# Sorted v of three batches: natural-layout sort and a re-tiling by way of DRAM in place of TensorE transposes

## The chip, the cores and the metric

The kernel runs on one core of one Trainium2 chip. The metric is the device time of one run in microseconds (us), given as the median of several runs. Profiles are of one run each, and their span is some 2 us shorter than that run's time, as it counts from the first to the last instruction.

## The reference

```python
# q, k, v: (4, 8, 768, 64); sort_net: (4, 8, 8, 8); w_in (512, 2048), w_out (2048, 512)
P = sort_net                        # 5 rounds of exp and row/column normalisation
k_sorted = einsum('bhij,bhjcd->bhicd', P, k_blocks)    # 8 blocks of 96 rows
v_sorted = einsum('bhij,bhjcd->bhicd', P, v_blocks)
scores = q_block @ k_sorted_block.T / 8                # block by block
out = softmax(scores) @ v_sorted_block
x = out with heads side by side                        # (3072, 512)
y = square(relu(x @ w_in)) @ w_out                     # the feed-forward part
```

Attention-times-v needs each sorted v block with its 96 rows on the partitions. The loads put 6 neighbouring rows of v side by side on one partition, so partition (j, c) holds rows 6c to 6c+5 of block j.

## The kernel before

A plan on the host orders the work of TensorE, ScalarE and VectorE once and for all: the attention pieces of four batches are woven between chunks of feed-forward matmuls. Batch 0 runs partly ahead. A head pair ("unit") of a later batch does this for v:

```python
def s_sort(u, t, due=0, early=False):          # t = 1: k, t = 2: v
    for a in range(NA):                        # 6
        for h in range(2):
            nc.tensor.matmul(                  # output transposed: head dim on partitions
                out=tp[64 * h:64 * (h + 1), a, :],
                lhsT=src[:, 2 * u.hp + h, D * a:D * (a + 1)],
                rhs=w_all[...])                # the sorting matrix moves
    # evicted to ksT or vsT
...
def s_vt(u, due=0):                            # v only: eight transposes back
    for n in range(u.ni):
        nc.tensor.transpose(out=vbp[:, n, :], in_=u.vsT[...], identity=ident)
    # evicted to vs, the right operand of attention-times-v (s_av)
...
def load(b, t, h0, n, p=slice(0, 128)):        # bulk loads, cast to bf16, issued by GpSimd
    ...                                        # for b > 1 they wait until batch b-2 is read out
```

In the profiles `tp` is the sort's output, `vbp` the transposes', `scp` the scores, `oup` attention-times-v, `xtp` the transposes of the attention output, `hp` the up- and `op` the down-projection.

The softmax here doesn't subtract the row's maximum and nothing guards it: scores larger than these inputs give would overflow.

Of the kernel before, what the change touches and what calls it, by code (L numbers as in the profile page):

```python
# [8 lines left out]
FP32 = mybir.dt.float32  # L9
BF16 = mybir.dt.bfloat16  # L10
# [32 lines left out]
class Plan:  # L43
# [1 line left out]



    TAIL = {"PE": 0.0, "ACT": 0.09, "DVE": 0.06, "POOL": 0.0, "DMA": 0.0, "SP": 0.0}
    HOP = 0.06

    def __init__(self):
# [60 lines left out]
def kernel(  # L112
# [10 lines left out]
    nc = tc.nc  # L123
# [24 lines left out]


    ctx.enter_context(tc.manual_schedule(engines={  # L150
        mybir.EngineType.PE, mybir.EngineType.DVE, mybir.EngineType.Activation}))

    plan = Plan()
    r1, r2, rf, rh1, rh2, rob = Ring(1), Ring(2), Ring(3), Ring(3), Ring(2), Ring(3)
    rqT, rao, rks, ret = Ring(6), Ring(3), Ring(3), Ring(4)
    AD = ("ACT", "DVE")

    def cost_f(n):
        return (0.17 + 0.82e-3 * n, 0.15 + 1.04e-3 * n)
# [26 lines left out]

    ksT_r, vsT_r, et_r, vs_r = [], [], [], []
    for n in range(3):
        for r, name in ((ksT_r, "ksT"), (vsT_r, "vsT")):
            sT = const.tile([128, 2, HS + 32], BF16, name=f"{name}{n}")  # L190
            nc.vector.memset(sT[:, :, HS:HS + 32], 0.0)
            r.append(sT)
        vs = const.tile([96, NB, 2, 66], BF16, name=f"vs{n}")
        nc.vector.memset(vs[:, :, :, D:D + 1], 1.0)
        vs_r.append(vs)
    for n in range(4):
        et = const.tile([96, 2, HS + 32], BF16, name=f"et{n}")
        nc.vector.memset(et[:, :, HS:HS + 32], 0.0)
        et_r.append(et)
# [46 lines left out]
        t = slice(NT // 4 * g, NT // 4 * (g + 1))  # L246
        dma(("w_out", g), 1.05, lambda t=t: (w_out_bf[:, t, :], w_out_r[:, t, :]))
    for g in range(2):
        for t in (1, 2, 0):
            load(1, t, HP * g, HP)  # L250


# [136 lines left out]
    def s_sort(u, t, due=0, early=False):  # L389

        st = {}

        def mm(e):
            src = qkv[u.b][t]
            if early:
                tp = psf.tile([128, 512], FP32, tag="pf", name="tp")
                tp = tp[:, 0:NA * u.ni * C0].rearrange("p (a x) -> p a x", a=NA)
            else:
                tp = ps2.tile([128, NA, u.ni * C0], FP32, tag="p2", name="tp")
            st["p"] = tp  # L400
            for a in range(NA):
                for h in range(2):
                    nc.tensor.matmul(  # L403
                        out=tp[64 * h:64 * (h + 1), a, :],
                        lhsT=src[:, 2 * u.hp + h, D * a:D * (a + 1)],
                        rhs=w_all[:, H * u.b + 2 * u.hp + h, u.i0:u.i0 + u.ni, :]
                        .rearrange("p i c -> p (i c)"),
                        start=True, stop=True)

        def ev(e):  # L410
            h0 = u.halves[0]
            copy(e, (u.ksT if t == 1 else u.vsT)[:, h0:h0 + len(u.halves), 0:HS]
                 .rearrange("p h (x a) -> p h x a", a=NA),
                 st["p"].rearrange("p a (h x) -> p h x a", x=NQ * C0))

        h0 = 2 * u.hp
        dep = landed[u.b, t, h0 if u.b == 0 else HP * (h0 // HP), 0]
        ring = rf if early else r2
        s2, old = ring.take()
        pe = plan.add("PE", 0.385 if u.full else 0.27, mm,  # L420
                      [dep, built[H * u.b + h0], built[H * u.b + h0 + 1]] + old, due)
        readers[u.b].append(pe)
        op = plan.add(AD, cost_f(NA * C0 * u.ni), ev, [pe] + u.old)
        ring.use(s2, pe, op)
        return op

    def s_sc(u, due=0):

        u.exps = {}
        u.et, last = {}, []  # L430
        for hf in u.halves:
            st = {}

            def mm(e, hf=hf, st=st):
                qT = tiles["qT", u.b, u.hp]
                st["p"] = scp = ps2.tile([128, 2, 512], FP32, tag="p2", name="scp")
                for n in range(NQ):
                    for h in range(2):
                        nc.tensor.matmul(  # L439
                            out=scp[:, h, BLK * n:BLK * (n + 1)],  # L440
                            lhsT=u.ksT[64 * h:64 * (h + 1), hf, BLK * n:BLK * n + 128],
                            rhs=qT[64 * h:64 * (h + 1), NQ * hf + n, :, :]
                            .rearrange("p a c -> p (a c)"),
                            start=True, stop=True)

            s2, old = r2.take()
            u.et[hf], olde = ret.take()
            pe = plan.add("PE", 0.25, mm, [u.k_op, u.q_op] + old, due)
            r2.use(s2, pe)
            rqT.use(qTs[u.b, u.hp], pe)  # L450
            last.append(pe)
            u.exps[hf] = []
            for h in range(2):
                def ex(e, h=h, st=st, et=et_r[u.et[hf]]):
                    nc.scalar.activation(  # L455
                        out=et[:, h, 0:HS].rearrange("p (n c a) -> p n c a", c=C0, a=NA),
                        in_=st["p"][0:96, h, 0:HS].rearrange("p (n a c) -> p n c a", c=C0, a=NA),
                        func=AF.Exp, scale=scale)
                op = plan.add("ACT", cost_f(HS)[0], ex, [pe] + olde)
                r2.use(s2, op)  # L460
                u.exps[hf].append(op)
        u.sc_pe = last

    def s_vt(u, due=0):

        st = {}

        def mm(e):
            st["p"] = vbp = ps1.tile([128, u.ni, 128], BF16, tag="p1", name="vbp")
            for n in range(u.ni):  # L470
                i = u.i0 + n
                nc.tensor.transpose(  # L472
                    out=vbp[:, n, :],
                    in_=u.vsT[:, i // NQ, BLK * (i % NQ):BLK * (i % NQ) + 128],
                    identity=ident)

        def ev(e):
            copy(e, u.vs[:, u.i0:u.i0 + u.ni, :, 0:D],
                 st["p"][0:96].rearrange("p n (e d) -> p n e d", d=D))

        s1, old = r1.take()
        pe = plan.add("PE", 0.446 if u.full else 0.22, mm, [u.v_op] + old, due)
        u.vs_op = plan.add(AD, cost_b(128 * u.ni), ev, [pe] + u.old)
        r1.use(s1, pe, u.vs_op)
        rks.use(u.n, pe, *u.sc_pe)

    def s_av(u, due=0):
        nao, olda = rao.take()
        u.norms = []
        for hf in u.halves:  # L490
            st = {}

            def mm(e, hf=hf, st=st):
                if hf == u.halves[0]:
                    u.ao = att.tile([96, u.ni, 2, D], BF16, tag="ao", name="ao", bufs=3)
                st["p"] = oup = ps2.tile([128, 2, 512], FP32, tag="p2", name="oup")
                for n in range(NQ):
                    for h in range(2):
                        nc.tensor.matmul(  # L499
                            out=oup[:, h, 66 * n:66 * n + D + 1],  # L500
                            lhsT=et_r[u.et[hf]][:, h, BLK * n:BLK * n + 128],
                            rhs=u.vs[:, NQ * hf + n, h, 0:D + 1],
                            start=True, stop=True)

            def norm(e, st=st, n0=NQ * hf - u.i0):
# [12 lines left out]
            op = plan.add("DVE", 0.9, norm, [pe])  # L518
            r2.use(s2, pe, op)
            ret.use(u.et[hf], pe)  # L520
            rks.use(u.n, pe)
            u.norms.append(op)
        u.nao = nao

# [123 lines left out]
    def lay(b, halves, c0, c1):  # L648
        step = (c1 - c0) / (HP + 0.9)
        for hp in range(HP):  # L650
            c = c0 + step * hp
            box = {}

            def open_(due, b=b, hp=hp, box=box):
                u = box["u"] = Unit(b, hp, halves)
                u.q_op = s_q(b, hp, C0 * u.i0, C0 * (u.i0 + u.ni), due)
                if b > 0:
                    build_w(H * b + 2 * hp, 2, pt, kops[b - 1, hp])
                u.k_op = kops[b, hp] = s_sort(u, 1, due)
                u.v_op = s_sort(u, 2, due)  # L660

            for f, s in ((0.0, open_),
                         (0.35, lambda due, box=box: s_sc(box["u"], due)),
                         (0.5, lambda due, box=box: s_vt(box["u"], due)),
                         (0.75, lambda due, box=box: s_av(box["u"], due)),
                         (1.2, lambda due, box=box: s_xt(box["u"], due))):
                todo.append((c + step * f, len(todo), s, b))

    lay(0, (1,), 0, n_up)
    for b, (c0, c1) in enumerate(((n_up, 2 * n_up), (2 * n_up, 4 * n_up), (4 * n_up, 6 * n_up)), 1):  # L670
# [2 lines left out]
    for due, _, stage, b in sorted(todo, key=lambda x: x[:2]):  # L673
        if b > 1 and not readers[b]:
            for g in range(2):
                for t in (1, 2, 0):
                    load(b, t, HP * g, HP)
        stage(int(due))
    for g in range(n_tok // HS):
# [41 lines left out]
```

## Time and profile before

| | before |
|---|---|
| time, median | 241.75 us (241.41 to 242.11, 3 runs); 241.88 with the run beside the changed kernel |
| span of the profiled run | 238.9 us (that run's time was 241.00 us, below the four in the row above) |
| TensorE busy | 230.5 us (96%) |
| VectorE, ScalarE busy | 51% each |
| bulk loads (software queue) | 13.63 MB, of which the later batches' run until about 62 us and from 73 to 90 us |

The prediction below shows the lines and how they are read.

### The profile page before, as it was taken

The page shows a single profiled execution, that of the slowest core. Times are in us where ns is not written, and L with a number is a line of the kernel's source. Part 1 is how long each engine was busy: PE and PEld are TensorE (multiplying, and loading weights), DVE is VectorE, ACT ScalarE, POOL GpSimd, SP SyncE. Part 2 cuts the span into 40 slices and gives each one's busy share as a digit, 9 for nine tenths or more (in the row PEclk, how much of TensorE's full clock was granted, in tenths as well). Part 3 has the DMA queues.
Part 4 walks back from the last instruction along what each step waited for, and adds up shares of the span by engine and source line. Part 5 has one row for each costly group of instructions (what it writes and reads, how often), then busy time and mean ns, then how long its engine had stood idle before and what let it go on. Part 6 is the DMA issues. An engine that isn't in the chain of part 4 may idle for free.

```text
span 238.9 us, 5867 instructions
## 1 busy us (share of the span) xinstructions
PE 230.5 (96%) x2485; PEld 138.1 (58%) x2501; DVE 121.4 (51%) x322; ACT 123.0 (51%) x256; POOL 27.0 (11%) x41
## 2 busy tenths in 40 slices
PE   7899999999999999999999999999999999999993
PEld 2777665556675556655665456655665456446541
DVE  6677777327785347744676037643666025105400
ACT  4365675237885247724674147723674147227510
POOL 8843221500006000000000000000000000000000
PEclk9999999999999999999999999999999999999999
DMA  6999999999405990011100120011100120011012
GB/s 81 193 204 207 206 207 206 201 241 222 76 3 68 220 238 9 3 44 47 45 3 0 44 91 0 3 44 47 44 3 1 47 88 1 19 72 44 0 44 88
DMA packets 20489, 20.30 MB, mean 85 GB/s; under 512 B 1008, under 2 KB 17392, under 8 KB 20464
## 3 DMA queue, kind: packets, MB, share of 16 engines
q0 software_dynamic: 16960, 13.63, 36.8%
q1 hardware_dynamic: 3504, 6.30, 7.2%
q8 instruction: 19, 0.31, 0.5%
q14 instruction: 6, 0.05, 0.1%
HBM read 27.27 MB, written 6.29 MB: 140 GB/s over the span
## 4 chain that ended last, share of the span: by engine, by line
PE 91%; DVE 4%; ACT 2%; issue 1%; POOL 0%; POOLq 0%
PE hp L562 35%; PE op L590 34%; PE tp L403 5%; PE vbp L472 3%; PE qtp L361 3%; PE oup L499 3%; PE scp L439 3%; PE xtp L531 3%; ACT qT L166 1%; DVE p_sb L266 1%; PE fill L283 0%; DVE vs L168 0%; ACT h L570 0%; DVE rs L265 0%; POOL qb L212 0%
## 5 line engine op out<-in xcount | busy, mean ns | idle before, releaser
L562 PE MATMUL hp<-xT,w_in_bf 128*128 128x384 bf16 x512 | 92.8, 326 | 0.0
L590 PE MATMUL op<-w_out_bf,h 128*128 128x512 bf16 x368 | 86.2, 379 | 1.0 <-issue 0.3
L570 ACT ACTIVATE h<-hp 128x384 bf16<-128x384 f32 x128 | 62.3, 494 | 26.1 <-PE hp L562 25.4
L573 DVE TENSOR_TENSOR h<-h 128x384 bf16<-128x384 bf16 x128 | 43.9, 354 | 37.2 <-ACT h L570 36.7
L562 PEld LDWEIGHTS <-w_in_bf 128*128 128x128 bf16 x512 | 46.4, 98 | 28.1
L590 PEld LDWEIGHTS <-h 128*128 128x128 bf16 x384 | 36.1, 98 | 39.7
L166 ACT COPY ob<-op 128x512 f32<-128x512 f32 x24 | 14.1, 586 | 57.5 <-PE op L590 57.5
L455 ACT ACTIVATE et<-scp 96x384 bf16<-96x384 f32 x64 | 26.4, 490 | 6.7 <-PE scp L439 6.7
L509 DVE TENSOR_TENSOR ao<-oup,rec 96x512 bf16<-96x512 f32 x32 | 22.0, 687 | 1.1
L168 DVE COPY vs<-vbp 96x1024 bf16<-96x1024 bf16 (+1 forms) x20 | 11.6, 580 | 19.5 <-PE vbp L472 19.4
L168 DVE COPY qT<-qtp 128x768 bf16<-128x768 bf16 (+1 forms) x15 | 7.3, 489 | 18.9 <-PE qtp L361 18.4
L166 ACT CAST ksT<-tp 128x768 bf16<-128x768 f32 (+1 forms) x17 | 11.7, 686 | 9.9 <-PE tp L403 9.6
L168 DVE COPY xT<-xtp 128x768 bf16<-128x768 bf16 (+1 forms) x16 | 7.9, 496 | 13.3 <-PE xtp L531 12.8
L283 PE MATMUL fill<-ones 128*128 128x128 bf16 (+1 forms) x108 | 12.0, 255 | 1.5 <-DVE ones L185 1.5
L499 PEld LDWEIGHTS <-et 96*128 96x128 bf16 x256 | 10.7, 98 | 3.1 <-ACT h L570 0.6
L168 DVE CAST vsT<-tp 128x768 bf16<-128x768 f32 (+1 forms) x14 | 11.8, 840 | 0.8
L499 PE MATMUL oup<-vs,et 96*128 96x65 bf16 x256 | 11.6, 193 | 0.2 <-DVE vs L168 0.2
L361 PEld LDWEIGHTS <-qb 128*64 128x64 bf16 (+1 forms) x240 | 6.9, 109 | 7.1 <-issue 5.8
L508 DVE RECIPROCAL rec<-oup 96x8 f32<-96x8 f32 x32 | 6.4, 199 | 8.3 <-PE oup L499 8.1
L472 PE MATMUL vbp<-ident,vsT 128*128 128x128 bf16 x128 | 10.5, 219 | 0.0
L212 POOL DMA_DIRECT2D qb<-in_q_dram x8 | 6.0, 747 | 39.1 <-PE qtp L361 33.3
L361 PE MATMUL qtp<-ident,qb 128*64 128x128 bf16 (+1 forms) x240 | 9.3, 212 | 0.8 <-DVE qT L168 0.4
(48 smaller groups left out, 130.5 us busy)
## 6 DMA issues: line engine op xcount, KB each, us to landing
out_dram<-ob SPq DMA_DIRECT2D x24, 256.0 KB, 2.0
qb<-in_q_dram POOLq DMA_DIRECT2D x8, 384.0 KB, 12.4
kb<-in_k_dram POOLq DMA_DIRECT2D x6, 384.0 KB, 15.1
vb<-in_v_dram POOLq DMA_DIRECT2D x6, 384.0 KB, 16.3
w_in_bf<-in_moe_w_in_dram POOLq DMA_DIRECT2D x4, 512.0 KB, 13.2
w_out_bf<-in_moe_w_out_dram POOLq DMA_DIRECT2D x4, 512.0 KB, 19.3
kb<-in_k_dram POOLq DMA_DIRECT2D x4, 192.0 KB, 6.1
vb<-in_v_dram POOLq DMA_DIRECT2D x4, 192.0 KB, 6.4
```

What stands on the lines that cost most here:

```text
L166: nc.scalar.copy(out=out, in_=in_)
L168: nc.vector.tensor_copy(out=out, in_=in_)
L283: nc.tensor.matmul(out=tiles["fill"][:, 0:w], lhsT=ones[:, 0:128], rhs=ones[:, 0:w], start=True, stop=True)
L361: nc.tensor.transpose(out=t["p"][64 * h:64 * (h + 1), a, :], in_=qb[p0:p1, 2 * hp + h, D * a:D * (a + 1)], identity=ident[p0:p1, p0:p1])
L455: nc.scalar.activation(out=et[:, h, 0:HS].rearrange("p (n c a) -> p n c a", c=C0, a=NA), in_=st["p"][0:96, h, 0:HS].rearrange("p (n a c) - ...
L472: nc.tensor.transpose(out=vbp[:, n, :], in_=u.vsT[:, i // NQ, BLK * (i % NQ):BLK * (i % NQ) + 128], identity=ident)
L499: nc.tensor.matmul(out=oup[:, h, 66 * n:66 * n + D + 1], lhsT=et_r[u.et[hf]][:, h, BLK * n:BLK * n + 128], rhs=u.vs[:, NQ * hf + n, h, 0:D ...
L509: nc.vector.tensor_tensor(out=u.ao[:, n0:n0 + NQ, :, :].rearrange("p n e d -> p e n d"), in0=ov[:, :, :, 0:D], in1=rec[:, :, :, None].to_b ...
L562: nc.tensor.matmul(out=t["hp", nt][:, 0:HS], lhsT=w_in_bf[:, kc, 128 * nt:128 * (nt + 1)], rhs=xT[:, kc, t0:t0 + HS], start=(kc == 0), sto ...
L570: nc.scalar.activation(out=t["h1", nt], in_=t["hp", nt][:, 0:HS], func=AF.Relu)
L573: nc.vector.tensor_tensor(out=t["h2"][:, nt, :], in0=t["h1", nt], in1=t["h1", nt], op=ALU.mult)
L590: nc.tensor.matmul(out=t["op", mt], lhsT=t["h2"][:, nt, 128 * mt:128 * (mt + 1)], rhs=w_out_bf[:, nt, :], start=(nt == 0), stop=(nt == NT ...
```

## The change

The intent is to take the eight transposes per unit off TensorE, which is the bound. For batches 1 to 3 the sorting matrix becomes the stationary operand and v moves in its natural layout. The result is written to DRAM and read back with the block rows on the partitions. A block holds two units (four heads).

```diff
+    def s_vn(b, g, due):
+        for hp in (2 * g, 2 * g + 1):
+            for h in range(2):
+                nc.tensor.matmul(out=st["p"][:, h, 0:NA * D],
+                    lhsT=w_all[:, H * b + 2 * hp + h, :, :]...,      # 128 columns stationary
+                    rhs=qkv[b][2][:, 2 * hp + h, :], ...)            # 384 columns moving
+            # evicted to vn, then:
+        nc.sync.dma_start(out=v_way[b, g], in_=vn ...)               # 396 KB
+        nc.sync.dma_start(out=vb_r[w] ...,                           # 768 pieces of 528 B
+                          in_=v_way[b, g].rearrange("(i c) a x -> (c a) i x", c=C0))
 ...
-            for t in (1, 2, 0):
+            for t in (2, 1, 0):                                      # v is loaded first
 ...
+            if b > 0 and hp % 2 == 0:
+                todo.append((max(c - 7, 0), len(todo), v_first, b))  # 7 chunks ahead
-                u.v_op = s_sort(u, 2, due)
+                if b == 0:
+                    u.v_op = s_sort(u, 2, due)
```

The sync engine's order, too, is now fixed by the plan, which counts 2.3 us for a write and 2.6 us for a read.

More of the change, by code (lines that the diff above doesn't have):

```diff
@@ L43 @@
 class Plan:
-    TAIL = {"PE": 0.0, "ACT": 0.09, "DVE": 0.06, "POOL": 0.0, "DMA": 0.0, "SP": 0.0}
+    TAIL = {"PE": 0.0, "ACT": 0.09, "DVE": 0.06, "POOL": 0.0, "DMA": 0.0, "SP": 0.0, "WAY": 0.0}
     HOP = 0.06
@@ L150 @@
     ctx.enter_context(tc.manual_schedule(engines={
-        mybir.EngineType.PE, mybir.EngineType.DVE, mybir.EngineType.Activation}))
+        mybir.EngineType.PE, mybir.EngineType.DVE, mybir.EngineType.Activation,
+        mybir.EngineType.SP}))
     plan = Plan()
+    rvn, rvb = Ring(2), Ring(3)
     r1, r2, rf, rh1, rh2, rob = Ring(1), Ring(2), Ring(3), Ring(3), Ring(2), Ring(3)
@@ L188 @@
     for n in range(3):
-        for r, name in ((ksT_r, "ksT"), (vsT_r, "vsT")):
-            sT = const.tile([128, 2, HS + 32], BF16, name=f"{name}{n}")
+        for r, name, hs in ((ksT_r, "ksT", 2), (vsT_r, "vsT", 1)):
+            sT = const.tile([128, hs, HS + 32], BF16, name=f"{name}{n}")
             nc.vector.memset(sT[:, :, HS:HS + 32], 0.0)
             r.append(sT)
-        vs = const.tile([96, NB, 2, 66], BF16, name=f"vs{n}")
+        vs = const.tile([96, NQ, 2, 66], BF16, name=f"vs{n}")
         nc.vector.memset(vs[:, :, :, D:D + 1], 1.0)
         vs_r.append(vs)
+    vn_r, vb_r = [], []
+    for n in range(2):
+        vn = const.tile([128, NA, HP, 66], BF16, name=f"vn{n}")
+        nc.vector.memset(vn[:, :, :, D:66], 1.0)
+        vn_r.append(vn)
+    for n in range(3):
+        vb_r.append(const.tile([96, NB, HP, 66], BF16, name=f"vblk{n}"))
+    v_way = nc.dram_tensor("v_way", (B, 2, 128, NA, HP * 66), BF16, kind="Internal").ap()
     for n in range(4):
@@ L410, in ev @@
         def ev(e):
-            h0 = u.halves[0]
+            h0 = u.halves[0] if t == 1 else 0
             copy(e, (u.ksT if t == 1 else u.vsT)[:, h0:h0 + len(u.halves), 0:HS]
@@ L429, in s_sc @@
         u.exps = {}
-        u.et, last = {}, []
+        u.et = {}
         for hf in u.halves:
@@ L450, in s_sc @@
             rqT.use(qTs[u.b, u.hp], pe)
-            last.append(pe)
+            rks.use(u.n, pe)
             u.exps[hf] = []
@@ L461, in s_sc @@
                 u.exps[hf].append(op)
-        u.sc_pe = last
     def s_vt(u, due=0):
@@ L473, in mm @@
                     out=vbp[:, n, :],
-                    in_=u.vsT[:, i // NQ, BLK * (i % NQ):BLK * (i % NQ) + 128],
+                    in_=u.vsT[:, 0, BLK * (i % NQ):BLK * (i % NQ) + 128],
                     identity=ident)
         def ev(e):
-            copy(e, u.vs[:, u.i0:u.i0 + u.ni, :, 0:D],
+            copy(e, u.vs[:, :, :, 0:D],
                  st["p"][0:96].rearrange("p n (e d) -> p n e d", d=D))
@@ L484, in s_vt, with mm, ev, write @@
         r1.use(s1, pe, u.vs_op)
-        rks.use(u.n, pe, *u.sc_pe)
+        rks.use(u.n, pe)
+    v_blk = {}
+    def s_vn(b, g, due):
+        m, oldm = rvn.take()
+        evs = []
+        for hp in (2 * g, 2 * g + 1):
+            st = {}
+            def mm(e, hp=hp, st=st):
+                st["p"] = ps2.tile([128, 2, 512], FP32, tag="p2", name="vnp")
+                for h in range(2):
+                    nc.tensor.matmul(
+                        out=st["p"][:, h, 0:NA * D],
+                        lhsT=w_all[:, H * b + 2 * hp + h, :, :].rearrange("p i c -> p (i c)"),
+                        rhs=qkv[b][2][:, 2 * hp + h, :],
+                        start=True, stop=True)
+            def ev(e, hp=hp, st=st):
+                h0 = 2 * (hp % 2)
+                copy(e, vn_r[m][:, :, h0:h0 + 2, 0:D],
+                     st["p"][:, :, 0:NA * D].rearrange("p e (a d) -> p a e d", d=D))
+            s2, old = r2.take()
+            h0 = H * b + 2 * hp
+            pe = plan.add("PE", 0.34, mm, [landed[b, 2, HP * g, 0], built[h0], built[h0 + 1]]
+                          + old, due)
+            readers[b].append(pe)
+            op = plan.add(AD, cost_f(2 * NA * D), ev, [pe] + oldm)
+            r2.use(s2, pe, op)
+            evs.append(op)
+        def write(e):
+            nc.sync.dma_start(out=v_way[b, g], in_=vn_r[m].rearrange("p a h x -> p a (h x)"))
+        w, oldw = rvb.take()
+        def read(e):
+            nc.sync.dma_start(
+                out=vb_r[w].rearrange("p i h x -> p i (h x)"),
+                in_=v_way[b, g].rearrange("(i c) a x -> (c a) i x", c=C0))
+        wr = plan.add("SP", 0.1, write, evs)
+        there = plan.add("WAY", 2.3, lambda e: None, [wr])
+        rd = plan.add("SP", 0.1, read, [there] + oldw)
+        back = plan.add("WAY", 2.6, lambda e: None, [rd])
+        rvn.use(m, *evs, there)
+        rvb.use(w, back)
+        v_blk[b, g] = w, back
     def s_av(u, due=0):
         nao, olda = rao.take()
+        if u.b > 0:
+            w, u.vs_op = v_blk[u.b, u.hp // 2]
         u.norms = []
@@ L501, in mm @@
                             lhsT=et_r[u.et[hf]][:, h, BLK * n:BLK * n + 128],
-                            rhs=u.vs[:, NQ * hf + n, h, 0:D + 1],
+                            rhs=(u.vs[:, n, h, 0:D + 1] if u.b == 0 else
+                                 vb_r[w][:, NQ * hf + n, 2 * (u.hp % 2) + h, 0:D + 1]),
                             start=True, stop=True)
@@ L520, in s_av @@
             ret.use(u.et[hf], pe)
-            rks.use(u.n, pe)
+            if u.b == 0:
+                rks.use(u.n, pe)
+            else:
+                rvb.use(w, pe)
             u.norms.append(op)
@@ L656, in open_, with v_first @@
                 u.q_op = s_q(b, hp, C0 * u.i0, C0 * (u.i0 + u.ni), due)
-                if b > 0:
-                    build_w(H * b + 2 * hp, 2, pt, kops[b - 1, hp])
                 u.k_op = kops[b, hp] = s_sort(u, 1, due)
-                u.v_op = s_sort(u, 2, due)
+                if b == 0:
+                    u.v_op = s_sort(u, 2, due)
+            if b > 0 and hp % 2 == 0:
+                def v_first(due, b=b, g=hp // 2):
+                    for x in (2 * g, 2 * g + 1):
+                        build_w(H * b + 2 * x, 2, pt, kops[b - 1, x])
+                    s_vn(b, g, due)
+                todo.append((max(c - 7, 0), len(todo), v_first, b))
             for f, s in ((0.0, open_),
                          (0.35, lambda due, box=box: s_sc(box["u"], due)),
-                         (0.5, lambda due, box=box: s_vt(box["u"], due)),
+                         (0.5, (lambda due, box=box: s_vt(box["u"], due)) if b == 0 else None),
                          (0.75, lambda due, box=box: s_av(box["u"], due)),
                          (1.2, lambda due, box=box: s_xt(box["u"], due))):
-                todo.append((c + step * f, len(todo), s, b))
+                if s:
+                    todo.append((c + step * f, len(todo), s, b))
     lay(0, (1,), 0, n_up)
@@ L675 @@
             for g in range(2):
-                for t in (1, 2, 0):
+                for t in (2, 1, 0):
                     load(b, t, HP * g, HP)
```

## The prediction

> **What bounds the kernel now.** I read the page's busy line first, then the chain that ended last, then the chain in order of time, then the groups by form, and last the DMA views.
>
> ```profile
> PE 230.5 (96%) x2485; PEld 138.1 (58%) x2501; DVE 121.4 (51%) x322; ACT 123.0 (51%) x256; POOL 27.0 (11%) x41
> PE 91%; DVE 4%; ACT 2%; issue 1%; POOL 0%; POOLq 0%
> ```
>
> TensorE (PE) is busy 96% of the 238.9 us span and is 91% of the chain. VectorE and ScalarE are half idle. So a piece of TensorE work that goes away shortens the run by its own length, and relief for VectorE is worth nothing by itself. The length must be read from the chain, because a matmul's own duration (219 ns) is a latency that overlaps its neighbours.
>
> ```profile
> 52.14 0.67 PE tp L403 x24
> 54.66 0.55 PE vbp L472 x8
> 56.51 0.51 PE oup L499 x16
> 90.72 0.45 PE vbp L472 x8
> 91.16 1.95 PE hp L562 x12
> 93.11 0.51 PE oup L499 x16
> 96.03 0.67 PE tp L403 x24
> 96.70 1.41 PE hp L562 x8
> ```
>
> The columns are start, length, engine, output tile, line and count. One head pair of a later batch takes 0.67 us for the sorts of k and v together (24 matmuls), so 0.335 us for v. The eight re-tiling transposes (vbp) take 0.45 us, sometimes 0.55. Twelve up-projection matmuls of 384 columns take 1.95 us, 0.1625 us each.
>
> ```profile
> L472 PE MATMUL vbp<-ident,vsT 128*128 128x128 bf16 x128 | 10.5, 219 | 0.0
> L168 DVE COPY vs<-vbp 96x1024 bf16<-96x1024 bf16 x12 | 8.2, 686 | 16.1 <-PE vbp L472 16.0
> L168 DVE CAST vsT<-tp 128x768 bf16<-128x768 f32 x10 | 9.5, 954 | 0.6
> 50.00:60.00 10.00, 10.00 (x153) 6.50 (x152) 6.36 (x13) 6.20 (x13) 0.00 (x0) 1.00 1.28 226
> 100.00:110.00 10.00, 9.79 (x105) 5.59 (x102) 4.87 (x11) 3.56 (x8) 0.00 (x0) 1.00 0.08 28
> 44.99 7.67 SPq L606 DMA_DIRECT2D out_dram<-ob  x3
> DMA to landing us min/median/max: 5.5/5.5/5.5
> q1 hardware_dynamic: 102, 0.21, 63.0%
> q0 software_dynamic: 106, 0.08, 52.0%
> ```
>
> The first three are groups by form. The next two are rows of the table by stretch; the last numbers are granted clock, DMA share and GB/s. The DMA engines are saturated at 50 to 60 us and nearly idle at 100 to 110 us. The last four concern the output stores: three are issued from 44.99 us on, the first lands 5.5 us later (the median of all 24 is 2.0), and between 56 and 57 us the store queue and the load queue moved 102 and 106 packets. This decides my forecast.
>
> **What the Trainium skill says.** "TensorE: Matmul & The Clock Gate", section "Back-to-back issue gap", gives N/2.4 + 2.5 ns for a warm matmul of N columns: 55.8 ns for 128 and 162.5 ns for 384. The trace agrees: 0.45/8 = 56 ns and 1.95/12 = 162.5 ns. The same page, "What's actually happening" in Part 1, has a clock gate that halves the clock after an idle window of about 3.4 us. Before, the granted clock is 1.00 in every 10 us stretch, so nothing shows it here. "DMA: Bandwidth & Descriptors", "Queues, rings and completion order", says each DMA engine round-robins between its queues; the 102 against 106 packets agree. The same page, "Two DMAs through the same engine are not ordered", says a DMA that reads what another wrote has to wait for that one's completion semaphore. So the new write and read are serial, each with its full latency; no pair of this kind is in the trace of before.
>
> **The change, part by part.** There are 3 later batches of 4 head pairs, 12 units.
> - *Removed on TensorE.* The v sort is 12 matmuls of 128 columns onto half-width outputs, which run in pairs: 0.335 us per unit. The eight transposes are 0.45 us, in two units 0.55. Removed: 12 x 0.335 = 4.0 us and 10 x 0.45 + 2 x 0.55 = 5.6 us, together 9.6 us.
> - *Added on TensorE.* Two matmuls per head pair, the 128-wide sorting matrix stationary and 384 columns moving: 2 x 0.1625 = 0.325 us, times 12 = 3.9 us.
> - *Net on TensorE.* 9.6 - 3.9 = 5.7 us less. Nearly all is the transposes; turning the sort round is worth 0.1 us. The switch cost that I read after the sort (8 up matmuls take 1.41 us, where 8 x 0.1625 = 1.30) stays, as the k sort stays.
> - *VectorE and ScalarE.* The 12 copies out of vbp go (8.2 us). The evictions of sorted v are as large as before (768 f32 columns: 0.80 us on ScalarE, 0.95 on VectorE). Building the sorting matrices only moves. No path is set here.
> - *DMA.* Six writes and six reads, one pair for two units. A write is 128 partitions x 6 x 4 x 66 x 2 B = 405 KB in rows of 3,168 B, a read the same bytes in 96 x 8 = 768 pieces of 528 B. Total 4.9 MB more beside 20.3 MB. Where engines idle, an estimate from the 256 KB store (2.0 us) is some 2.5 us for the write and 3 to 4 for the read.
> - *Moved.* The v work of two units starts 7 chunks of feed-forward work ahead of the first. VectorE and ScalarE then need about 1.7 us before the write can be issued.
>
> **Does the way hide?** TensorE takes its instructions in the fixed order of the host's plan, which counts 2.3 us for the write and 2.6 for the read. If the block is late at the first attention-times-v (oup), TensorE stands still.
> - *Batches 2 and 3, and the second half of batch 1:* from v's sort to its use there are 14 us or more of other work (for batch 1's second half from about 57 us to 71 us; for the first half of batch 2 from 78.8 to 93.1). With idle DMA 1.7 + 2.5 + 4 = 8 us is needed. Only the first half of batch 2 lies beside loads (75 to 90 us): about 0 to 1 us at risk.
> - *First half of batch 1:* chunk 21 is at about 45.0 us, where before the last attention-times-v of batch 0 stands. Its v was landed (the first k load of batch 1, whose place v takes, was issued at 19.85 us and landed 20.0 later). Sort and evict end at 46.8 us. The store of the same kind in this stretch needed 5.3 to 5.8 us; its bytes begin to move only 3.3 us after the issue, and it moves for 1.5. The write, 1.5 times as large, should land about 5.8 us on, at 52.7. The read is issued then. Its 48 pieces per DMA engine take turns with load packets of about 80 ns: 48 x (30 + 80) = 5.3 us if they alternate strictly, 1.5 us if not (30 ns is my estimate from the 14 ns that the small packets of the first load took). So it lands at 52.8 + 3.3 + 1.5 to 5.3 + 0.7, that is 58.3 to 62.1 us.
> - TensorE wants it at about 56.3 us: before, oup was at 56.51, and 0.34 + 0.55 of v work goes in front of it while 0.65 comes in. The wait is 2.0 to 5.8 us, middle about 4.
>
> Sum: 241.75 - 5.7 + 4.0 (this wait) + 0.2 (first half of batch 2) = 240.25. I predict **240.2 us**.
>
> **The rivals.**
> - *The transfer is hidden.* Then the whole 5.7 us comes out: 236.0 us, 2.4% less. For it: the author gave 7 chunks of lead, and some 11 us lie between sort and use, twice what the plan counts. Against it: every output store in a loaded stretch took 4.8 to 6.3 us instead of 2.0.
> - *The wait swallows the gain.* The read moves at the strict alternation's pace, TensorE idles near 6 us, and the clock gate named above takes another 1 to 2 us after an idle time of over 3.4 us. Then 241.75 - 5.7 + 6 + 1.5 = 243.5 us. For it: the 102 against 106 packets. Against: a granted clock of 1.00 throughout, and the small pieces may be bundled.
> - *Another engine becomes the bound.* The sync engine now blocks on each write before it issues the read, and output stores queue behind it; three output buffers and 3 stores per half batch leave room. VectorE loses 8 us. This makes nothing of the time, at most 0.3 us.
>
> **Range and chances.** The removal is sure to about 0.4 us. What spreads is the wait, 0 to 6 us and perhaps the gate: 236.0 to 243.5. I give 236.3 to 243.3 for 8 in 10. Faster by over 2% means below 236.9 us, which needs a wait under 0.9 us: 0.20. Slower by over 2% means above 246.6: 0.03. Within 2%: 0.77.
>
> **What would show it.** Right, if the changed profile has no vbp on 128x1024 outputs, 24 up-type 384-column v matmuls taking about 0.65 us per four in the chain, TensorE busy time near 225 us, and one idle time of 2 to 6 us before the first oup of batch 1 near 56 us that a DMA read ends, with write and read there landing in 5 to 9 us each against 2 to 4 later on. Wrong, if that idle time is absent (then the run is near 236), if late reads stall TensorE in the quiet stretches too, or if v's sort in the new layout costs more than 0.16 us per matmul.

## The result, and the profile after

The changed kernel took 244.49 us (243.24 to 244.77, 4 runs) against 241.88 us before. The ratio is 1.010, with a 95% interval of 1.006 to 1.014. A ratio here is the mean time of one kernel's fast runs over that of the other's in the same rounds, so it is not quite the ratio of the medians quoted. The kernel is a little slower: 1% is within the 2% called "same", but it is clear of the noise, and outside my range.

The busy line and the chain's shares by engine, of the changed kernel:

```profile
PE 228.3 (94%) x2269; PEld 132.7 (55%) x2285; DVE 111.9 (46%) x310; ACT 123.4 (51%) x258; POOL 27.0 (11%) x41
PE 83%; DMA 10%; DVE 3%; ACT 2%; issue 1%; SPq 0%
```

TensorE's share of the chain fell from 91% to 83%, and a tenth of the chain is now DMA. The timeline of the sync engine (SPq), of TensorE and of GpSimd (POOL) shows where; its columns are start, length, engine, line, instruction, and in brackets the idle time before it and what ended it:

```profile
47.56 0.33 SPq L531 DMA_DIRECT2D v_way<-vn  x1
53.30 0.34 SPq L536 DMA_DIRECT2D vblk<-v_way  x1
62.51 0.60 PE L562 MATMUL oup<-vblk,et 96*128 96x65 bf16 x8 [5.51 <-DMA vblk<-v_way]
62.91 1.47 PE L629 MATMUL hp<-xT,w_in_bf 128*128 128x384 bf16 x4
68.67 1.48 POOL L224 DMA_DIRECT2D vb<-in_v_dram  x2 [22.44 <-PE vnp L510]
69.44 0.33 SPq L531 DMA_DIRECT2D v_way<-vn  x1
79.62 0.41 PE L562 MATMUL oup<-vblk,et 96*128 96x65 bf16 x8 [1.31 <-DMA vblk<-v_way]
```

TensorE stands still for 5.51 us before the first attention-times-v of batch 1, and for 1.31 us before that of its third unit. Both times the block read back from DRAM ends it. Just before the second block's write, GpSimd issues two loads of v for batch 3, which waited only until the new sort had read v of batch 1 out.

The chain in order of time, again of the changed kernel:

```profile
45.82 0.66 PE vnp L510 x4
47.56 5.73 DMA v_way<-vn
53.30 9.07 DMA vblk<-v_way
63.10 1.28 PE hp L629 x4
121.48 1.95 PE hp L629 x12
```

The first block needs 5.73 us out and 9.07 us back. And four `hp` matmuls right after the wait take 1.28 us, 0.32 each, where later twelve take 1.95 us, 0.1625 each. They run at half speed. The table by stretch (last three numbers: granted clock, DMA share, GB/s) has the reason:

```profile
60.00:70.00 10.00, 7.49 (x66) 4.42 (x67) 4.53 (x10) 3.12 (x6) 1.33 (x2) 0.66 0.57 106
```

The granted clock fell to 0.66 on average over these 10 us. What the read was doing meanwhile is in the queue lines of the DMA view for 57 to 62 us (packets, MB, share; q0 carries the bulk loads, q1 the transfers that the sync engine issues):

```profile
q0 software_dynamic: 830, 0.62, 79.0%
q1 hardware_dynamic: 822, 0.50, 44.5%
```

822 pieces of the sync engine's queue, 761 of them the read's, went between 830 packets of the bulk loads. That they took turns one for one is seen in a short stretch: from 59.00 to 59.10 us the DMA view has 16 packets of each queue, one of each for every one of the 16 DMA engines.

The turns are not the whole of the 9.07 us. The records of the trace have the read's first piece at 56.94 us and the end of its last at 62.02: 3.6 us passed before anything moved, and the 768 pieces took 5.1 us. In a quiet stretch (the read issued at 113.36 us, 3.9 us in all) the two are 1.2 and 2.3 us.

**The account**, from the two traces (span 238.9 to 242.7 us, +3.8). These are traces of a quick run of the old kernel (241.00 us) and of the slowest of the new one (244.77); the medians differ by 2.6 only, so this is the account of these two runs:

| term | us | from |
|---|---|---|
| later start | +0.6 | the first `hp` is at 23.89 us before, 24.51 after. The first 14 warm-up matmuls took 4.54 and 5.63 us. Other traces have anything from 4.5 to 6.1, so this is spread and not the change |
| work off TensorE | -6.3 | as the run without waits (e8) shows it: 5.7 counted |
| first wait | +5.5 | the line at 62.51 |
| slow clock after it | +2.7 | from 62.51 to 68.30 us stand 16 `oup`, 12 `hp` and 4 `vnp` matmuls, which at full speed take 0.51 + 1.95 + 0.65 = 3.1 us. In e4's trace the same work takes 3.4 (four of the `hp` stand later there and are counted at 0.65), which makes this term 2.4 |
| second wait | +1.3 | the line at 79.62 |

Their sum is +3.8.

### The profile page after: what moved, and what is told of

Read it like the earlier page. It is cut to its first block, busy times and chain, and to the rows that moved or that the text cites. A ratio compares the mean times of both kernels' runs of the same rounds, so it can differ in the third digit from the quotient of the medians.

```text
span 242.7 us, 5456 instructions
## 1 busy us (share of the span) xinstructions
PE 228.3 (94%) x2269; PEld 132.7 (55%) x2285; DVE 111.9 (46%) x310; ACT 123.4 (51%) x258; POOL 27.0 (11%) x41
## 4 chain that ended last, share of the span: by engine, by line
PE 83%; DMA 10%; DVE 3%; ACT 2%; issue 1%; SPq 0%
PE hp L629 32%; PE op L657 31%; DMA vblk<-v_way 5%; DMA v_way<-vn 5%; PE oup L562 3%; PE qtp L373 3%; PE tp L415 3%; PE fill L295 3%; PE scp L451 3%; PE xtp L598 2%; PE vnp L510 2%; PE vbp L483 1%; ACT qT L168 1%; ACT h L637 0%; DVE vn L170 0%
## 5 line engine op out<-in xcount | busy, mean ns | idle before, releaser
L629 PE MATMUL hp<-xT,w_in_bf 128*128 128x384 bf16 x512 | 94.6, 331 | 0.0
L637 ACT ACTIVATE h<-hp 128x384 bf16<-128x384 f32 x128 | 61.1, 496 | 30.6 <-PE hp L629 29.9
L168 ACT COPY ob<-op 128x512 f32<-128x512 f32 x23 | 13.5, 585 | 52.7 <-PE op L657 52.7
L562 PEld LDWEIGHTS <-et 96*128 96x128 bf16 x256 | 11.8, 99 | 11.1 <-issue 6.2
L562 PE MATMUL oup<-vblk,et 96*128 96x65 bf16 x192 | 9.6, 197 | 6.8 <-DMA vblk<-v_way 6.8
L168 ACT CAST ksT<-tp 128x768 bf16<-128x768 f32 (+1 forms) x16 | 10.9, 679 | 9.4 <-PE tp L415 9.1
L295 PE MATMUL fill<-ones 128*128 128x128 bf16 (+1 forms) x108 | 13.1, 268 | 1.5 <-DVE ones L187 1.5
L224 POOL DMA_DIRECT2D vb<-in_v_dram x10 | 7.5, 747 | 25.2 <-PE vnp L510 22.4
L295 PEld LDWEIGHTS <-ones 128*128 128x128 bf16 x108 | 7.3, 103 | 5.1 <-issue 3.2
L598 PEld LDWEIGHTS <-ao 96*128 96x128 bf16 x128 | 7.6, 97 | 3.6 <-issue 0.2
L415 PE MATMUL tp<-w_all,kb 128*64 128x128 bf16 (+1 forms) x240 | 9.0, 211 | 0.2 <-ACT ksT L168 0.2
```

Of the source, the lines that this page charges most:

```text
L168: nc.scalar.copy(out=out, in_=in_)
L295: nc.tensor.matmul(out=tiles["fill"][:, 0:w], lhsT=ones[:, 0:128], rhs=ones[:, 0:w], start=True, stop=True)
L415: nc.tensor.matmul(out=tp[64 * h:64 * (h + 1), a, :], lhsT=src[:, 2 * u.hp + h, D * a:D * (a + 1)], rhs=w_all[:, H * u.b + 2 * u.hp + h, u ...
L562: nc.tensor.matmul(out=oup[:, h, 66 * n:66 * n + D + 1], lhsT=et_r[u.et[hf]][:, h, BLK * n:BLK * n + 128], rhs=(u.vs[:, n, h, 0:D + 1] if ...
L629: nc.tensor.matmul(out=t["hp", nt][:, 0:HS], lhsT=w_in_bf[:, kc, 128 * nt:128 * (nt + 1)], rhs=xT[:, kc, t0:t0 + HS], start=(kc == 0), sto ...
L637: nc.scalar.activation(out=t["h1", nt], in_=t["hp", nt][:, 0:HS], func=AF.Relu)
```

## The experiments

My theory was that the block's way through DRAM is late only where bulk loads run beside it, that its pieces take turns with the loads' packets, and that a long standstill costs a second time through the clock. The rivals were that two serial transfers are too slow by themselves, that the new sort gives less on TensorE than counted, and that the waits are of another kind (the sync queue's order, the aftermath of the first wait). e1 to e4 ran on one chip beside before's 241.26 us (7 runs); e8, e5 and e6 ran on one chip beside 241.64 us (7 runs). The changed kernel itself was not timed again there, so a step from its 244.49 us compares different rounds. All results were correct.

**e1: bulk loads of batches 2 and 3 held back.**

```diff
+            if gate:      # block (1,1): one element of it goes into the load's destination first
+                nc.gpsimd.tensor_copy(out=dst[0:1, 0:1, 0:1],
+                                      in_=vb_r[gate[0]][0:1, 0, 0:1, 0:1])
...
-                    load(b, t, HP * g, HP)
+                    load(b, t, HP * g, HP, gate=v_blk[1, 1] if b in (2, 3) else None)
```

> One edit to the changed kernel: the loads of batches 2 and 3 are held back until batch 1's second block has come back from DRAM (a one-element copy out of the block into each load's destination, so the load has to wait). My theory (the way through DRAM is late because its pieces take turns with the bulk loads; the standstill then costs a second time through the clock): the write of batch 1's first half still meets batch 1's own last loads and lands in 3 to 5 us instead of 5.7, the read is alone and lands in about 4 us instead of 9.1, so the block is there before TensorE asks at about 57 us. No wait, clock 1.00 in every stretch, and the whole TensorE saving shows: 241.9 - 5.7 = 236.2 us, up to 236.8 if the 0.6 us later start belongs to the change. Rival (two serial transfers with their receipts and the blocked sync queue are too slow by themselves, loads or not): a wait of 3 us or more stays, 239 us or more. Second rival (sorting in natural layout costs TensorE more than I think): no waits, but 238 us or more.

Measured: 240.33 us, ratio 0.995 (0.993 to 0.998). Batch 1 did as expected: its first block went out in 3.3 us and came back in 3.8, and TensorE waited for neither block. So the way is not too slow by itself. But the time was missed by 4 us, as a new wait stood in batch 2 (timeline):

```profile
94.05 0.41 PE L566 MATMUL oup<-vblk,et 96*128 96x65 bf16 x8 [4.01 <-DMA vblk<-v_way]
95.57 3.39 PE L633 MATMUL hp<-xT,w_in_bf 128*128 128x384 bf16 x12
```

Twelve `hp` matmuls took 3.39 us after it, again the slow clock (0.83 over 90 to 100 us). I had pushed the loads of batches 2 and 3 into one train, from 68 to beyond 90 us, and batch 2's first block now met it: 6.6 us out, 9.2 back.

**e2: only batch 3's loads held back.**

```diff
+                    load(b, t, HP * g, HP, gate=v_blk[1, 1] if b in (3,) else None)
```

(The gate itself as in e1.)

> One edit: only the loads of batch 3 are held back until batch 1's second block is back; batch 2's loads stay where they are. My theory: the second, smaller wait (1.3 us before the third head pair of batch 1) is caused by batch 3's v loads, which the change lets start at 68.7 us because v of batch 1 is read out earlier than before. It goes, the first wait and the slow clock after it stay: 244.4 - 1.3 = 243.1 us; write and read of batch 1's second block in 2.4 and 4 us instead of 5.8 and 4.2. Rival (that wait is only the aftermath of the first, everything being late): it stays, 244.4 us.

Measured: 243.05 us, ratio 1.008 (1.004 to 1.011). The second block went out in 2.4 us and came back in 3.6, and its wait is gone; the first wait (5.53 us) and the slow clock are still there. The second wait was therefore made by batch 3's v loads, which the change itself had let start earlier. The time agrees with the 243.1 expected, but it doesn't show the step by itself: by the ratios to before it is 0.6 us, within the noise. From the first `hp` to the end the traces have 218.2 us in the changed kernel and 217.0 here.

**e3: more lead.**

```diff
-                todo.append((max(c - 7, 0), len(todo), v_first, b))
+                todo.append((max(c - 12, 0), len(todo), v_first, b))
```

> One number: v's sort starts 12 chunks ahead instead of 7; loads as in the changed kernel. My theory: the first write is issued near 43 us, still under load, lands near 49, the read near 58, TensorE wants it near 57: a wait of 1 to 1.5 us, too short for the clock to fall; the second block has time enough. 237 to 238 us. Write and read keep their loaded durations of about 6 and 9 us. Rival (the block's way is short of a resource that more lead doesn't give, such as the sync queue's order): the wait stays over 4 us.

Measured: 242.25 us (241.23 to 243.74), ratio 1.004 (0.9995 to 1.0084): no difference from before is shown, and my number was wrong. The wait was 4.08 us, not 1 to 1.5, and the granted clock fell to 0.83 over 60 to 70 us. (The trace is of the fastest of the four runs, with a mean clock of 0.993; the other three have 0.986, as low as the changed kernel's 0.984 to 0.985.) The sync engine's two issues and the wait, in the timeline:

```profile
45.26 0.33 SPq L531 DMA_DIRECT2D v_way<-vn  x1
51.42 0.34 SPq L536 DMA_DIRECT2D vblk<-v_way  x1
61.22 0.41 PE L562 MATMUL oup<-vblk,et 96*128 96x65 bf16 x8 [4.08 <-DMA vblk<-v_way]
```

Five chunks more of lead moved the write from 47.56 only to 45.26 us. The durations stayed at their loaded size (6.1 and 9.7 us) as the theory had it. The lead also let batch 3's v loads start at 52.53 us in place of 68.67, and the second block then took 11.1 us out and 6.9 back, though TensorE did not wait for it. Why the sort didn't start sooner I did not test: it began at 43.36 us, some 3 us after v can have landed (the load in the same place of the order had landed at 39.9 us before). Lead bought 2.3 us of earlier issue and 1.4 us of wait, so it is a weak cure here.

**e4: the standstill filled.**

```diff
+        if (u.b, u.hp) == (1, 0):          # before the first attention-times-v of batch 1
+            def busy(e):
+                t = ps2.tile([128, 2, 512], FP32, tag="p2", name="busy")
+                for _ in range(90):
+                    nc.tensor.matmul(out=t[:, 0, 0:128], lhsT=ones[:, 0:128],
+                                     rhs=ones[:, 0:128], start=True, stop=True)
```

> One edit: 90 matmuls of 128 columns on constant data (90 x 56 ns = 5.0 us) stand in TensorE's order just before the first attention-times-v of batch 1, where it waits 5.5 us. They make no result. My theory: they fill the standstill, so the clock is not lowered and the 6 us after it run at full speed: the wait shrinks to about 0.5 us, granted clock 1.00 from 60 to 70 us, and the run is 2.8 us shorter, 241.6 us. Rival (matmuls after 62 us are slow for another reason, such as the bulk transfers): they stay at 0.32 us per 384 columns and the time stays at 244.4.

Measured: 242.38 us, ratio 1.004 (1.002 to 1.006). TensorE's timeline there:

```profile
56.39 5.19 PE L557 MATMUL busy<-ones 128*128 128x128 bf16 x90
62.06 0.66 PE L570 MATMUL oup<-vblk,et 96*128 96x65 bf16 x16 [0.48 <-DMA vblk<-v_way]
62.56 1.46 PE L637 MATMUL hp<-xT,w_in_bf 128*128 128x384 bf16 x8
```

With useless work in the gap, the clock stayed at 1.00 in every stretch and eight `hp` matmuls after it ran at full speed. So the slow matmuls were an effect of the standstill and not of the transfers, which were still there. The gain was 2.1 us between the medians and 1.5 us by the ratios, less than the 2.8 expected. From the first `hp` to the end the traces have 218.2 us in the changed kernel and 215.6 here, 2.6 us less; of these, 0.4 stem from a shorter second wait (0.87 us). The direction is shown, and a size of some 2.1 us by the traces.

**e8: each batch's loads held back until the batch before has its last block.**

```diff
-                    load(b, t, HP * g, HP, gate=v_blk[1, 1] if b in (2, 3) else None)
+                    load(b, t, HP * g, HP, gate=v_blk[b - 1, 1])
```

(Shown against e1.)

> As the first run with held loads, with one word changed: batch 2's loads wait for batch 1's second block as there, but batch 3's loads now wait for batch 2's second block instead of following batch 2's at once. In that first run the waits of batch 1 were gone and a new one of 4.0 us stood in batch 2, whose first block went out (6.6 us) and came back (9.2 us) beside the loads of batch 3. My theory (only bulk loads beside a block's way make it late): batch 2's first block now meets only the end of batch 2's own loads, lands in time, no TensorE wait on any block is left, the granted clock is 1.00 in every stretch after the start, and the whole TensorE saving shows: 241.3 - 5.7 = 235.6 us, up to 236.3 with a slow start; ratio to before 0.976 to 0.980. Rival (the natural-layout sort gives less on TensorE than the trace's rows say, or the held loads come too late for their own batches): no block waits, but 238 us or more, or new waits for q, k, v loads.

Measured: 234.81 us (234.56 to 235.49), ratio 0.973 (0.971 to 0.975). This beats both kernels. The busy line of its page:

```profile
PE 227.2 (97%) x2285; PEld 131.6 (56%) x2285; DVE 111.7 (48%) x310; ACT 123.4 (53%) x258; POOL 28.4 (12%) x53
```

The first attention-times-v of batch 1 in its timeline:

```profile
57.34 0.41 PE L566 MATMUL oup<-vblk,et 96*128 96x65 bf16 x8
```

And the time to landing of the first block's write and of its read, from the view of the DRAM tensor:

```profile
DMA to landing us min/median/max: 3.5/3.5/3.5
DMA to landing us min/median/max: 4.0/4.0/4.0
```

No bracket stands behind `oup`: TensorE did not wait. The write took 3.5 us in place of 5.7, the read 4.0 in place of 9.1. The only wait for a block left in the trace is 0.2 us in batch 2, whose first block's write still meets the end of batch 2's own loads (6.0 us). Its read took 5.9 us with hardly a load beside it (8 load packets between 85 and 88 us), which my theory does not explain. The time lies below my range: from the first `hp` matmul to the end the trace shows 238.9 - 23.89 = 215.0 us before and 233.7 - 25.01 = 208.7 us here, 6.3 us less, where I had counted 5.7 (the medians of the runs differ by 6.8). Of the 0.6 more, 0.2 is a wait for the copy out of the transposes that stood in before's trace; the rest I did not locate.

**e5: batch 1 back on the transposes.**

```diff
+    def turned(b, hp):
+        return b <= 1            # the change: b == 0
```

> One part of the change undone: batch 1 goes back to the transposes (as batch 0 always does), only batches 2 and 3 go by way of DRAM; no load is held back. My theory: the long wait, the slow clock and the second wait all belonged to batch 1 and go; 8 units save 8 x 0.47 = 3.7 us; batch 2's first block still goes beside batch 3's loads and may be 0 to 1.5 us late: 237.5 to 239 us. Rival (the loss lies in the way itself, in any batch): batch 2 shows a wait of over 3 us like batch 1's before, 241 us or more.

Measured: 238.64 us, ratio 0.988 (0.986 to 0.990). No wait for a block is left, and the loss is gone. So the whole loss belonged to batch 1. Batch 2's first block, beside batch 3's loads, took 6.3 and 5.9 us and was in time.

**e6: only the first two units of batch 1 back on the transposes.**

```diff
+        return b == 0 or (b == 1 and hp < 2)
```

(The rest as in e5.)

> A smaller part undone: only the first two head pairs of batch 1 go back to the transposes, the other ten units go by way of DRAM; no load is held back. My theory: the 5.5 us wait and the slow clock after it go; 10 units save 4.7 us; the second block of batch 1 has 14 us, of which write and read take some 10 beside the loads, so a wait of 0 to 1 us there, the same in batch 2: 236.6 to 238.5 us. Rival (the first block's lateness only hides that the second is as late): a wait of 4 us or more moves to the third head pair, with the slow clock behind it, 241 us or more.

Measured: 238.26 us, ratio 0.987 (0.984 to 0.989). One wait remained (timeline):

```profile
71.36 0.66 PE L565 MATMUL oup<-vblk,et 96*128 96x65 bf16 x16 [1.70 <-DMA vblk<-v_way]
```

It is 1.70 us, more than the 0 to 1 expected; again v loads of batch 3 were issued (61.66 us) while the block was on its way. The clock did not fall after it. The rival, a wait of 4 us or more, is out.

**e10: each block read back in two halves.** One single run (state unknown), for its profile.

```diff
+            for k in range(2):
+                nc.sync.dma_start(out=vb_r[w][:, :, 2 * k:2 * k + 2, :]...,
+                                  in_=v_way[b, g]....[:, :, 132 * k:132 * (k + 1)])
```

> One edit to the changed kernel: each block is read back by two transfers, one for each head pair, of 768 pieces of 264 B each, where one transfer had 768 pieces of 528 B. The first head pair of batch 1 needs only the first of the two. My theory (beside the loads a read is paced by its number of pieces, since pieces take turns with load packets one for one): the first read of batch 1 lands in about 8.5 to 9.3 us, hardly sooner than the 9.1 us of the whole block, although it carries half the bytes; the first wait stays at 5 to 5.5 us. In the quiet stretches the two reads land in about 3 to 5 us. Rival (a read is paced by its bytes): the first read lands in 6 to 7 us and the first wait shrinks to 2.5 to 3.5 us. What the second read does to the next head pair is not forecast.

Measured: 244.41 us. Time to landing of the first read of batch 1, from the view of the DRAM tensor:

```profile
DMA to landing us min/median/max: 8.6/8.6/8.6
```

The queue lines of the DMA view between 57 and 62 us:

```profile
q0 software_dynamic: 954, 0.71, 90.9%
q1 hardware_dynamic: 918, 0.24, 36.1%
```

Half the bytes in as many pieces took 8.6 us against 9.1, and the wait stayed at 5.08 us. The pieces again went one for one with the load packets (918 to 954; 902 of the 918 are pieces of the two reads) while they carried half as much (0.24 MB against 0.50). Once it moves, a read beside the loads is paced by its number of pieces. The 3.6 us before the first piece stood here too (first piece at 57.06 us, issue at 53.44); no run tested what makes them.

## Why the prediction was wrong

The step that failed is the cost of the block's way through DRAM, of which the sum held 4.0 + 0.2 us. The runs showed 5.5 us for the first wait, 2.7 us for the slow clock after it, 1.3 us for a second wait, and none in batch 2. With these, and the 6.3 us of e8 for the removal, the prediction's sum comes to 241.75 - 6.3 + 5.5 + 2.7 + 1.3 = 244.95 us, where 244.49 was measured.

- **The bound and the removal** were right. TensorE's removed work was worth its own length as soon as nothing else stood in its way (e8), 6.3 us where 5.7 were counted.
- **Where the wait would stand** was right: the first half of batch 1, the DMA read ending it. Write and read landed at 53.3 and 62.4 us, where I had 52.7 and 58.3 to 62.1.
- **The wait's size failed in the sum.** I took "middle about 4" of 2.0 to 5.8 us because I did not trust the strict alternation. The wait was 5.5 us. e10 and the packet counts show strict alternation, so the upper end was the one to take: I had 3.3 us before the first piece and 5.3 us for the pieces at most, and the trace has 3.6 and 5.1.
- **The clock was left out of the sum.** "TensorE: Matmul & The Clock Gate" of the Trainium skill, section "What's actually happening" in Part 1, was quoted, and the cost stood in a rival alone as "another 1 to 2 us", with the granted clock of 1.00 before as evidence against. That was no evidence, as TensorE had no such idle time before. The trace shows half speed for 5.4 us of work, 2.7 us lost; e4 shows that the standstill causes it. Waits of 1.3 and 1.7 us left the clock alone, waits of 4.0, 4.1, 5.1 (e10) and 5.5 us did not, which agrees with that page's window of about 3.4 us. The granted clock in half-microsecond stretches shows more: it stood at 0.50 for 3.4 us after the waits of 4.0 and 4.1 us, all of it work time. With the waits of 5.1 and 5.5 us it stood there for 6.8 us, of which 5.3 to 5.9 were work time, as the fall came before the wait was over.
- **"The second half of batch 1 has 14 us" failed** as a step. It took the loads' times from the kernel before. The change reads v of batch 1 out earlier, so its buffers come free and batch 3's v loads start at 68.67 us instead of 75.05 (for the first of them), beside that block. This cost 1.3 us and went with e2.
- **The first half of batch 2** was put at 0 to 1 us of risk, and there was no wait (4.5 us for its read).
- **The second rival** came nearest, with 243.5 us, as its mechanism is what the runs show. No run showed a loss from the sync queue's order or from VectorE, though none tested them alone.
- **Of the signs** named beforehand, TensorE's busy time failed: put near 225 us, it was 228.3. It is no measure of the gain here, as e8 had 227.2 and was yet 6.3 us shorter than before from the first `hp` to the end.
- The median lies 1.2 us above my range. The clock's 2.7 and the second wait's 1.3 us are the terms that were missing.

## What to carry to other kernels

When work moves from the bound engine to a DMA way, forecast the way from transfers that ran in the same stretch, piece by piece against the packets of whatever runs beside it, and look at which loads the change itself sets free there. If the way is late, moving the competing bulk loads behind it can be worth more than more lead: here 234.8 us instead of 242.3. And count an in-order TensorE's long standstill twice: once for the wait, once for the slow clock after it.

## What the Trainium skill lacked or had wrong

- "DMA: Bandwidth & Descriptors", "Queues, rings and completion order", has the round robin "at *packet* granularity", where a packet is a group of some 9 to 17 descriptors. In the records here the two queues alternated piece by piece: 822 pieces (761 of 528 B) against 830 load packets, 918 (902 of 264 B) against 954, and 16 against 16 within 0.1 us. The page has no rule for what follows: a read of 768 pieces took 9.1 us beside loads and mostly 3.6 to 4.3 us in quiet stretches, and half the bytes in as many pieces still 8.6 us.
- The same page has no figure for the delay before a transfer moves at all beside a saturated queue: the first output store of the kernel before moved its bytes only 3.5 us after its issue began and landed after 5.5 us, against 2.0 us in quiet stretches, and the first read of the changed kernel moved nothing for 3.6 us, against 1.2 us in a quiet stretch.
- No page that I read has the cost of a DRAM round trip of this size inside a kernel. Here 396 KB took mostly 2.3 to 2.6 us out and mostly 3.6 to 4.3 us back without loads beside it (three such reads took 5.0 to 5.9), and mostly 5.7 to 7.3 us out and up to 9.7 us back beside saturating loads.
- "TensorE: Matmul & The Clock Gate", "What's actually happening", has the window of about 3.4 us right for this case. It lets the clock come back after at least one busy window, and leaves open how long one wait costs: here the slow clock lasted 3.4 us with waits of 4.0 and 4.1 us, and 6.8 us with waits of 5.1 and 5.5 us, of which the changed kernel's cost 2.7 us.
